# Early idle products, key transposes, a split load of v and reordered ScalarE copies in a fused sketch-attention and GELU kernel

## Chip, cores and metric

The kernel runs on one core of one Trainium2 chip. The metric is the device time of one execution in microseconds (us). A core has TensorE (PE: matrix products and transposes, into PSUM), VectorE (DVE), ScalarE (ACT), GpSimd (POOL) and SyncE (SP, whose queue issues nearly all transfers here). Each engine works through its own instructions in order.

## What is computed

Polynomial-sketch attention on 4 batches x 4 heads x 1088 tokens x 32 features, followed by a two-layer block with exact GELU:

```python
def phi(x):
    a = np.einsum('rd,bhsd->bhsr', S1, x)
    b = np.einsum('rd,bhsd->bhsr', S2, x)
    return np.einsum('bhsi,bhsj->bhsij', a, b).reshape(*x.shape[:-1], r * r)
q_p, k_p = (phi(q), phi(k))                       # r = 8
kv = np.einsum('bhsf,bhsd->bhfd', k_p, v)
z = np.sum(k_p, axis=2)
num = np.einsum('bhsf,bhfd->bhsd', q_p, kv)
den = np.einsum('bhsf,bhf->bhs', q_p, z)[..., None] + 1e-06
x = (num / den)   # heads side by side: 4352 tokens x 128
h = x @ w_in      # 128 x 2048
g = 0.5 * h * (1.0 + erf(h * inv_sqrt2))
out = g @ w_out   # 2048 x 128
```

S1, S2, w_in and w_out arrive as 64-bit floats; the kernel makes 32-bit floats of them itself.

## The kernel before

**Tiling.** Each batch has 1024 main tokens, in two chunks of 512, and 64 remaining tokens. So there are 8 main chunks (n = 0 to 7, batch n // 2) and a ninth chunk of 256 with the remaining tokens of all batches. The hidden width is cut into 16 blocks of 128 (fi). w_in and w_out are held in five pieces of 256, 256, 512, 512 and 512 columns or rows, each with its own transfer and its own rounding.

**Order.** The last lines of the kernel tie every instruction to the one before it on the same engine, so each engine runs in the order of the text. An instruction that waits holds up all that stands behind it on its engine.

**Loads.** SP issues, in order: k of batch 0 in two halves (heads 0 and 2, then 1 and 3), q of chunk 0, v of batch 0 in one load of 512 KB, the remaining tokens' k for batches 0 and 2, the first piece of w_in, the remaining v of batch 0, q of chunk 1, the second piece of w_in, two pieces of w_out. `load_rest` issues all the rest later; its first load of w_in is held back by a one-element memset on POOL (L128).

**Prologue (L511 to L574).** All of batch 0's attention up to the first products is written out by hand:

- `keep_busy(n, ps)` multiplies a tile of zeros (`idle`) into part of a PSUM bank that nobody reads, n times, 256 columns each. These are the idle products. A float32 product shows as two MATMULs in the trace (x2), a transpose as one.
- `Rounding` turns a 64-bit tile into 32 bits: `low_words` (ACT, L209), `fields` (DVE, L213 bits_e and L215 bits_a), `exponents` (ACT, L221), `mantissas` (DVE L229, or with `by_pool` ACT L226 and POOL L227), `signs` (DVE, L234), `product` (L239, on DVE or POOL).
- `key_turn` transposes half of the keys with four PE transposes (L265) and copies them to SBUF (kT, L267, here by ACT). `sketches` transposes the rounded sketch matrices SR (L253) and makes S12, sT (DVE) and Srep (POOL).
- `key_features` multiplies kT by the sketches (L303), copies one factor with ACT (a_t, L316 or L313) and forms the outer products k_p (DVE L317; for one half POOL L314).
- `widen_v(b, r)` copies half of v's heads, those of r, into v_aug (POOL, L278). `kv_sum` accumulates k_p times v_aug (L336), `kv_sum_rem` does so for the remaining tokens (L343), `take_kv` and `turn_kv` give kz (L349, L352, L353).
- `query_turn(n)` makes qT (for chunk 0 with DVE, L367; for chunk 1 with four PE transposes and an ACT copy). `expand_products(n)` is four products of 512 columns (L376) into two pairs of banks; `expand_copy(n, g)`, g = 0 to 3, copies one factor with ACT (A_sb, L383); `expand_multiply(n, i)`, i = 0 or 1, takes copies 2i and 2i+1 and makes half of q_pT with two DVE multiplies (L397).
- `attend_by_token(n, banks)` is 32 small products (L442) of q_pT with kz, the second half of which reads what `expand_multiply(n, 1)` made; then DVE adds (L446), takes reciprocals (L447) and divides (L449) into x_tok. `turn_x` transposes x_tok on PE and copies it to xT.

**Main loop (L641).** A step t belongs to a pair (n, fi). `hidden` multiplies xT by a block of w_in into one of two banks h_ps (L466) and lets ACT take the gelu (g, L468). Two steps later `project` accumulates g times w_out into o_ps (L481). Steps 0 to 3 are fi = 0 to 3 of chunk 0, steps 4 to 7 the same of chunk 1, and so on in turn up to step 31; later chunks run through all 16 blocks each. In between, `slots[t]` holds other work, put there with `at(t, ...)` and run after `hidden` and ahead of `project` of that step. Chunk 1's remaining preparation lies in slots 0 to 3, its `turn_x` ahead of step 4.

Of the kernel before, what the change touches and what calls it, by code (L numbers as in the profile page):

```python
# [16 lines left out]
def kernel(  # L17
# [18 lines left out]
    pe, dve, act, pool, sp = nc.tensor, nc.vector, nc.scalar, nc.gpsimd, nc.sync  # L36
    B, H, S, D = q.shape
# [10 lines left out]
    CW = JC * 128  # L48
# [15 lines left out]
    def work_banks():  # L64

        return wps.tile([128, 2, CW], FP, name="w_ps")

    def work_bank():
        return work_banks()[:, 0]
# [4 lines left out]
    def hidden_bank():  # L74
        return hps.tile([128, CW], FP, name="h_ps")

    def out_bank():
        return ops.tile([128, CW], FP, name="o_ps")


    by_act, by_dve, by_pool = act.copy, dve.tensor_copy, pool.tensor_copy
# [12 lines left out]
    def load_main(eng, n, b, heads=slice(0, H)):  # L94
        eng.dma_start(out=main[n, b][:, heads],  # L95
                      in_=src_of[n][b, heads, 0:MAIN, :].rearrange("h (p j) d -> p h j d", j=J))
# [46 lines left out]
    for r in range(2):  # L143
        load_main(sp, "k", 0, slice(r, H, 2))
    load_q(0)
    load_main(sp, "v", 0)
    load_rem("k", 0)
    load_rem("k", 2)
    load_w_in(0)
# [42 lines left out]
    idle = big.tile([128, 256], FP, name="idle")  # L192
# [58 lines left out]
    def sketches():  # L251
        ps = work_bank()
        pe.transpose(ps[:, :2 * R], in_=SR, identity=ident[:2 * R, :2 * R])  # L253
        dve.tensor_mul(out=S12, in0=ps[:, None, :2 * R].broadcast_to([128, H, 2 * R]),
                       in1=mask4[:, :, None].broadcast_to([128, H, 2 * R]))
        dve.tensor_copy(out=sT, in_=ps[:, :2 * R])
        for i in range(2):
            src = sT[:, 0:R, None] if i == 0 else sT[:, None, R:2 * R]
            pool.tensor_copy(out=Srep[:, i], in_=src.broadcast_to([128, R, R]))
# [10 lines left out]
    def four_tokens(n, b, h, c):  # L270
        return main[n, b][:, h, c * JC:(c + 1) * JC, :].rearrange("p j d -> p (j d)")
# [4 lines left out]
    def widen_v(b, r):  # L276
        to = v_aug.rearrange("p (c r) j (s d) -> p c r j s d", r=2, s=2)[:, :, r, :, r, :]
        pool.tensor_copy(out=to, in_=main["v", b][:, r::2])  # L278
# [9 lines left out]
    def key_turn(b, r, ps, copy):  # L288
        kT[r] = transposed(ps, "kT", [four_tokens("k", b, h, c) for h in (r, r + 2) for c in range(NCH)], copy)
# [7 lines left out]
    def key_features(b, r, banks, by_pool=()):  # L297

        for i in range(2 * NCH):
            for c in range(2):  # L300
                for t in range(2):
                    at = i * 128 + c * 64
                    pe.matmul(banks[t][c * 64:(c + 1) * 64, i * 32:(i + 1) * 32],  # L303
                              lhsT=kT[r][t * 64:(t + 1) * 64, at:at + 64],
                              rhs=S12[t * 64:(t + 1) * 64, 2 * t:2 * t + 2].rearrange("p h r -> p (h r)"),
                              start=True, stop=True)

        k_p[b, r] = att.tile([128, 2, J, R, R], FP, name="k_p")
        a = att.tile([128, 2, J, 2 * R], FP, name="a_t")
        for t in (1, 0):  # L310
            ab = banks[t][:, :128].rearrange("p (n r) -> p n r", r=2 * R)
            if t in by_pool:
                act.copy(out=a[:, t], in_=ab)  # L313
                pool.tensor_mul(**spread(k_p[b, r][:, t], a[:, t, :, 0:R], a[:, t, :, R:2 * R]))  # L314
            else:
                act.copy(out=a[:, t, :, 0:R], in_=ab[:, :, 0:R])  # L316
                dve.tensor_mul(**spread(k_p[b, r][:, t], a[:, t, :, 0:R], ab[:, :, R:2 * R]))  # L317
# [13 lines left out]
    def kv_sum(b, ps, r):  # L331

        for i in range(J):
            ch, t, one = i // 4, i // 2 % 2, i % 2
            for c in range(NP):
                pe.matmul(ps[c * 64:(c + 1) * 64, r * F:(r + 1) * F], lhsT=v_aug[:, 2 * c + r, i, :],  # L336
                          rhs=k_p[b, r][:, t, c * 4 + ch * 2 + one].rearrange("p i j -> p (i j)"),
                          start=(r == 0 and i == 0), stop=False, skip_group_check=True)

    def kv_sum_rem(b, ps):  # L340
        for r in range(2):
            for c in range(NP):
                pe.matmul(ps[c * 64:(c + 1) * 64, r * F:(r + 1) * F], lhsT=v_rem_aug[b][:, 2 * c + r, :],  # L343
                          rhs=k_p_rem[b % 2][:, 2 * c + r].rearrange("p i j -> p (i j)"),
                          start=False, stop=True, skip_group_check=True)
# [13 lines left out]
    def query_turn(n, copy=by_act):  # L359


        if n == 1:
            turned = transposed(out_bank(), "qT", [q_sb[1][:, h].rearrange("p j d -> p (j d)") for h in range(H)], copy)
            qT[n] = turned.rearrange("p (h j t) -> p h j t", h=H, j=JC)
            return
        qT[n] = att.tile([128, H, width[n] // 128, D], FP, name="qT" if n < NMAIN else "qT_rem")
        dve.transpose(out=qT[n], in_=q_sb[n] if n < NMAIN else rem["q"].rearrange("p i h d -> p h i d"))  # L367
# [12 lines left out]
    def expand_copy(n, g):  # L380
        if g % 2 == 0:
            A[g // 2] = att.tile([128, 2, CW], FP, name="A_sb", bufs=2)
        act.copy(out=A[g // 2][F:, g % 2, :width[n]], in_=B_of[n][g // 2][:F, g % 2, :width[n]])  # L383
# [48 lines left out]
    def attend_by_token(n, banks):  # L432

        x_tok[n] = att.tile([128, JC, H, D], FP, name="x_tok", bufs=1)
        to = x_tok[n].rearrange("p j (c r) d -> p (j c) r d", r=2)
        den = att.tile([128, 2, JC * NP], FP, name="den_tok")
        for i in range(JC):
            for c in range(NP):
                for half in range(2):
                    for r in range(2):  # L440
                        rows, at, tok = slice(r * F, (r + 1) * F), (i * NP + c) * C, i * 128 + half * 64
                        pe.matmul(banks[r][half * 64:(half + 1) * 64, at:at + C], lhsT=qp[n][rows, c, tok:tok + 64],  # L442
                                  rhs=kz[n // NCH][rows, c, (0, D - 1)[r]:(C, 2 * D)[r]], start=True, stop=True)
        nd = [banks[r][:, :JC * NP * C].rearrange("p (g c) -> p g c", c=C) for r in range(2)]
        for r in range(2):
            dve.tensor_scalar(out=den[:, r], in0=nd[r][:, :, (D, 0)[r]], scalar1=1e-6, scalar2=None, op0=AX.add)  # L446
        dve.reciprocal(out=den, in_=den)  # L447
        for r in range(2):
            dve.tensor_mul(out=to[:, :, r], in0=nd[r][:, :, r:r + D],  # L449
                           in1=den[:, r, :, None].broadcast_to([128, JC * NP, D]))  # L450

    def turn_x(n, ps, copy):
        xT[n] = transposed(ps, "xT", [x_tok[n][:, j].rearrange("p h d -> p (h d)") for j in range(JC)], copy)
# [50 lines left out]
                         in_=oT[c * 32:(c + 1) * 32].rearrange("p n (m d) -> p (n m) d", d=32))  # L504


    def keep_busy(n, ps):
        for i in range(n):
            pe.matmul(ps[:, 256:512], lhsT=idle[:, 0:128], rhs=idle, start=True, stop=True)

    keep_busy(3, work_bank())  # L511
    r = Rounding(SR)
    r.low_words()
    r.fields()
    r.exponents()
    r.finish()
    key_turn(0, 0, hidden_bank(), by_act)
    sketches()
    query_turn(0)
    key_turn(0, 1, hidden_bank(), by_act)  # L520
    widen_v(0, 0)
    banks = [out_bank(), out_bank()]
    key_features(0, 0, banks)
    key_features(0, 1, [hidden_bank(), hidden_bank()], by_pool=(1,))
    widen_v(0, 1)
    widen_v_rem(0)
    expand_products(0)
# [10 lines left out]
    expand_copy(0, 3)  # L538
    expand_multiply(0, 1)
    kv_sum(0, kv_bank, 1)  # L540
    kv_sum_rem(0, kv_bank)
    w_in[0].exponents()
    take_kv(0, kv_bank, by_act)
# [9 lines left out]
    w_in[0].product(pool)  # L553
    w_in[1].low_words()
    w_in[1].exponents()
    keep_busy(1, hidden_bank())
    attend_by_token(0, [hidden_bank(), hidden_bank()])
    expand_products(1)
    keep_busy(1, out_bank())
    w_out = [Rounding(w) for w in w_out_sb[:2]]  # L560
    w_out[0].low_words()
    for g in range(2):
# [3 lines left out]
    w_in[1].product(pool)  # L566
    w_out[0].fields()
    turn_x(0, hidden_bank(), by_act)
    w_out[0].exponents()
    expand_multiply(1, 0)  # L570
    w_out[0].mantissas()
    w_out[0].signs()
    w_out[0].product(pool)
    w_out[1].fields()  # L574


    steps = [(n, fi) for f in range(0, NF, 4) for n in range(2) for fi in range(f, f + 4)]
# [3 lines left out]
    def at(t, f, *a):  # L581
        slots[t].append(lambda: f(*a))
# [25 lines left out]
        at(t, lambda: (r.append(Rounding(w)), r[0].low_words(), r[0].fields()))  # L608
        at(t + 1, lambda: (r[0].exponents(), r[0].finish()))

    at(0, lambda: (w_out[1].low_words(), w_out[1].exponents()))
    for g in range(2, 4):
        at(1, expand_copy, 1, g)
    at(1, expand_multiply, 1, 1)
    at(1, lambda: (w_out[1].mantissas(), w_out[1].signs(), w_out[1].product(pool)))
    at(3, lambda: attend_by_token(1, halves(work_banks())))
    for i, (t0, t1) in enumerate(((4, 6), (8, 10), (12, 20))):
        round_at(t0, w_in_sb[i + 2])
# [76 lines left out]
```

## Time and profile before

| | |
|---|---|
| runs | 294.57, 294.48, 296.11, 293.99 us; median 294.53 |
| profiled execution | 294.38 us |
| its span | 292.1 us |
| busy in the span | PE 282.5 us (97%), ACT 135.0 (46%), DVE 120.6 (41%), POOL 15.0 (5%) |
| granted PE clock | 0.998 of full speed on average |

The span is the time from the first to the last recorded instruction. PE is nearly always busy, so where it was idle matters. In stretches of the span (us), from the view that gives each engine's busy time by window:

| stretch | PE busy | DVE busy | ACT busy | POOL busy | transfer share |
|---|---|---|---|---|---|
| 0 to 3 | 1.80 | 1.75 | 1.27 | 1.78 | 0.34 |
| 3 to 6 | 2.48 | 1.78 | 1.31 | 0.04 | 0.86 |
| 6 to 9 | 2.67 | 2.28 | 1.55 | 1.04 | 0.98 |
| 9 to 12 | 2.70 | 2.93 | 2.88 | 2.00 | 0.82 |
| 12 to 15 | 2.24 | 2.80 | 1.37 | 0.00 | 0.00 |
| 15 to 18 | 2.66 | 2.36 | 2.84 | 1.83 | 0.23 |
| 18 to 21 | 2.55 | 2.92 | 1.64 | 0.55 | 0.96 |
| 21 to 24 | 2.83 | 1.52 | 2.92 | 0.54 | 0.99 |
| 24 to 27 | 2.15 | 2.87 | 0.22 | 0.72 | 1.06 |
| 27 to 30 | 2.33 | 0.36 | 1.28 | 0.00 | 1.10 |
| 30 to 33 | 3.00 | 1.37 | 1.92 | 1.54 | 0.79 |

The transfer share is the mean busy share of the 16 transfer engines (overlapping packets can put it over 1). TensorE's waits, summed by who ended them, are all in the first 29 us:

```text
PE w_ps L509 <- DVE idle L193: 1.2, 1, 1.2
PE o_ps L343 <- DVE k_p_rem L329: 1.0, 1, 1.0
PE h_ps L466 <- POOL w_in L239: 0.8, 1, 0.8
PE h_ps L466 <- ACT xT L267: 0.7, 1, 0.7
PE w_ps L253 <- DVE SR L239: 0.5, 1, 0.5
PE w_ps L265 <- DVE x_tok L449: 0.5, 1, 0.5
PE w_ps L442 <- DVE q_pT L397: 0.3, 1, 0.3
```

Each line names the instruction that waited, the one it waited for, and then the total, the number and the longest of these waits in us. A line such as `16.53 0.70 PE L509 MATMUL ... x2` in a timeline gives start, duration, engine, line, operation, what it writes and reads, and how many instructions are merged in it; square brackets name the idle time before it and its cause.

### The profile page before, as it was taken

How to read it: one execution, taken by the hardware profiler on the slowest of the kernel's cores; microseconds unless marked ns; L12 is line 12 of the kernel's file. 1: busy time of each engine (PE TensorE's matmuls, PEld its weight loads, DVE VectorE, ACT ScalarE, POOL GpSimd, SP SyncE). 2: the span in 40 equal slices, each digit the busy share in tenths (PEclk: the TensorE clock that was granted, in tenths of full speed). 3: DMA queues.
4: the chain of work that ended last, by engine and by line, in shares of the span. 5: the costliest groups of instructions: out<-in, count | busy, mean ns of one | idle time of the engine just before them, and what ended most of it. 6: DMA issues, size and time to landing. Idle time of an engine off the chain costs nothing.

```text
span 292.1 us, 3792 instructions
## 1 busy us (share of the span) xinstructions
PE 282.5 (97%) x1497; PEld 137.2 (47%) x1497; DVE 120.6 (41%) x186; ACT 135.0 (46%) x259; POOL 15.0 (5%) x45
## 2 busy tenths in 40 slices
PE   7887999999999999999999999999999999999994
PEld 5543445543443345533443345533443344444694
DVE  5985586344813284251713085242513161222000
ACT  4673674265435443256335543256336533443341
POOL 2340200110000000200000000000000000000000
PEclk9999999999999999999999999999999999999999
DMA  6569678100012000200002000200001000200010
GB/s 196 181 180 375 125 202 225 20 0 0 2 27 34 12 0 2 36 2 0 0 0 37 0 2 0 39 0 0 0 9 29 0 0 0 36 2 0 9 29 18
DMA packets 32561, 13.37 MB, mean 46 GB/s; under 512 B 21408, under 2 KB 31904, under 8 KB 32544
## 3 DMA queue, kind: packets, MB, share of 16 engines
q1 hardware_dynamic: 32304, 13.05, 17.3%
q8 instruction: 12, 0.20, 0.3%
q10 hardware_dynamic: 240, 0.08, 0.1%
q14 instruction: 5, 0.04, 0.0%
HBM read 10.90 MB, written 2.23 MB: 45 GB/s over the span
## 4 chain that ended last, share of the span: by engine, by line
PE 90%; DVE 4%; DMA 2%; SPq 1%; issue 1%; ACT 1%; ACTq 0%
PE h_ps L466 39%; PE o_ps L481 38%; PE o_ps L478 2%; PE w_ps L376 2%; PE w_ps L417 2%; PE w_ps L336 2%; DMA raw_w_in<-in_moe_w_in_dram 2%; DVE q_pT L397 1%; PE w_ps L265 1%; PE w_ps L303 1%; DVE bits_a L215 0%; SPq L95 0%; SPq L108 0%; PE h_ps L442 0%; DVE bits_e L234 0%
## 5 line engine op out<-in xcount | busy, mean ns | idle before, releaser
L468 ACT ACTIVATE g<-h_ps 128x512 f32<-128x512 f32 (+1 forms) x144 | 82.4, 573 | 130.3 <-PE h_ps L466 130.0
L466 PE MATMUL h_ps<-xT,w_in 128*128 128x512 f32 (+1 forms) x288 | 140.3, 569 | 1.5 <-POOL w_in L239 0.8
L481 PE MATMUL o_ps<-g,w_out 128*128 128x512 f32 x256 | 133.1, 601 | 0.2 <-POOL w_out L239 0.2
L466 PEld LDWEIGHTS h_ps<-xT,w_in 128*128 128x128 f32 x288 | 53.5, 190 | 63.9 <-issue 60.3
L481 PEld LDWEIGHTS o_ps<-g,w_out 128*128 128x128 f32 x256 | 46.2, 190 | 58.1 <-issue 56.5
L424 DVE RECIPROCAL den<-den 128x512 f32<-128x512 f32 (+1 forms) x7 | 21.9, 3124 | 44.0 <-ACT den L423 44.0
L397 DVE TENSOR_TENSOR q_pT<-A_sb,w_ps 64x512 f32<-64x512 f32 x32 | 22.1, 691 | 25.4 <-ACT A_sb L383 24.8
L491 DVE STREAM_TRANSPOSE oT<-o_ps 128x512 f32<-128x512 f32 x8 | 5.7, 717 | 43.9 <-PE o_ps L481 43.9
L383 ACT COPY A_sb<-w_ps 64x512 f32<-64x512 f32 (+1 forms) x36 | 17.7, 557 | 3.4 <-PE w_ps L376 3.2
L428 DVE TENSOR_TENSOR xT<-w_ps,den 32x512 f32<-32x512 f32 (+1 forms) x28 | 18.2, 649 | 1.0
L423 ACT ACTIVATE den<-w_ps 32x512 f32<-32x512 f32 (+1 forms) x28 | 15.6, 557 | 3.0 <-PE w_ps L417 2.7
L317 DVE TENSOR_TENSOR k_p<-a_t,w_ps 128x512 f32<-128x512 f32 x12 | 8.0, 686 | 6.5 <-ACT a_t L316 6.5
L478 PEld LDWEIGHTS o_ps<-w_out,g 128*128 128x128 f32 x64 | 9.3, 191 | 0.7
L278 POOL COPY v_aug<-v 128x512 f32<-128x512 f32 x8 | 4.9, 618 | 91.0 <-issue 62.0
L478 PE MATMUL o_ps<-w_out,g 128*128 128x128 f32 x64 | 9.4, 274 | 0.0
L376 PE MATMUL w_ps<-qT,Srep 32*128 32x512 f32 x64 | 9.1, 639 | 0.2 <-DVE qT L367 0.2
L229 DVE SCALAR_TENSOR_TENSOR bits_m<-bits_a,bits_low 128x512 f32<-128x512 uint32 (+2 forms) x10 | 5.7, 572 | 3.7 <-ACT bits_low L209 3.1
L417 PE MATMUL w_ps<-q_pT,kz 64*64 64x512 f32 (+1 forms) x80 | 7.2, 458 | 0.0
L221 ACT ACTIVATE bits_r<-bits_e,below 128x512 uint32<-128x512 uint32 (+2 forms) x11 | 6.7, 609 | 0.6 <-DVE bits_e L213 0.5
L336 PEld LDWEIGHTS w_ps<-k_p,v_aug 128*64 128x64 f32 x192 | 5.8, 138 | 2.3 <-issue 2.3
L336 PE MATMUL w_ps<-k_p,v_aug 128*64 128x64 f32 x192 | 6.3, 224 | 0.0
L267 DVE COPY kT<-w_ps 128x512 f32<-128x512 f32 x6 | 3.9, 685 | 4.5 <-PE w_ps L265 4.5
(119 smaller groups left out, 113.2 us busy)
## 6 DMA issues: line engine op xcount, KB each, us to landing
v<-in_v_dram SPq DMA_DIRECT2D x4, 512.0 KB, 6.8
raw_w_in<-in_moe_w_in_dram SPq DMA_DIRECT2D x3, 512.0 KB, 4.5
raw_w_out<-in_moe_w_out_dram SPq DMA_DIRECT2D x3, 512.0 KB, 7.5
k<-in_k_dram SPq DMA_DIRECT2D x3, 512.0 KB, 6.0
q<-in_q_dram SPq DMA_DIRECT2D x24, 64.0 KB, 4.7
out_dram<-oT SPq DMA_DIRECT2D x24, 64.0 KB, 2.2
k<-in_k_dram SPq DMA_DIRECT2D x2, 256.0 KB, 3.1
q<-in_q_dram SPq DMA_DIRECT2D x2, 256.0 KB, 4.9
```

The costliest lines, as they stand in the source:

```text
L336: pe.matmul(ps[c * 64:(c + 1) * 64, r * F:(r + 1) * F], lhsT=v_aug[:, 2 * c + r, i, :], rhs=k_p[b, r][:, t, c * 4 + ch * 2 + one].rearrang ...
L376: pe.matmul(B_of[n][g // 2][:, g % 2, :W], lhsT=Srep[rows].rearrange("p a i j -> p (a i j)"), rhs=qT[n][rows].rearrange("p h j t -> p (h j ...
L383: act.copy(out=A[g // 2][F:, g % 2, :width[n]], in_=B_of[n][g // 2][:F, g % 2, :width[n]])
L397: dve.tensor_mul(out=cols[r * F:(r + 1) * F], in0=a[:, :, r::2], in1=b[:, :, r::2])
L417: pe.matmul(banks[r][c * F:(c + 1) * F, c0:c1], lhsT=kz[b][r * F:(r + 1) * F, c, :], rhs=qp[n][r * F:(r + 1) * F, c, c0:c1], start=True, s ...
L423: act.activation(out=den[h * D:(h + 1) * D, :W], in_=banks[r][at:at + D, :W], func=ACT.Copy, bias=1e-6)
L424: dve.reciprocal(out=den[:, :W], in_=den[:, :W])
L428: dve.tensor_mul(out=xT[n][rows, :W], in0=banks[h % 2][rows, :W], in1=den[rows, :W])
L466: pe.matmul(ps[:, :W], lhsT=w_tile(w_in_sb, fi), rhs=xT[n][:, :W], start=True, stop=True)
L468: act.activation(out=g_of[n, fi][:, :W], in_=ps[:, :W], func=ACT.Gelu)
L478: pe.matmul(o_of[n][:, i * 128:(i + 1) * 128], lhsT=g[:, i * 128:(i + 1) * 128], rhs=w_tile(w_out_sb, fi), start=(first and i == 0), stop= ...
L481: pe.matmul(o_of[n], lhsT=w_tile(w_out_sb, fi), rhs=g, start=first, stop=final)
```

## The change

Five things are changed; the function bodies not shown stay as they are.

1. v of batch 0 is loaded in two transfers, heads 0 and 2 first, so that each is what one `widen_v` reads.
2. `key_turn(0, 1)` moves from behind `query_turn(0)` to ahead of `sketches()`.
3. `keep_busy` can take fewer columns. Three idle products of 128 columns come in around `key_features`, one of 256 ahead of `kv_sum_rem`; the one ahead of chunk 0's attention shrinks to 128, the one behind `expand_products(1)` becomes two, and one more follows the transposes of `turn_x(0)`.
4. ACT's copies g = 2 and 3 for chunk 1 move from step 1, behind two gelus: copy 2 into the prologue, copy 3 into step 0, behind the first gelu. The multiply that takes both moves to step 0.
5. The first piece of w_out takes its last product on DVE instead of POOL, directly behind its mantissas and signs. The second piece's low words move into the prologue, its fields and exponents to step 1, its mantissas, signs and product (POOL) to step 2.

```diff
     load_q(0)
-    load_main(sp, "v", 0)
+    for r in range(2):
+        load_main(sp, "v", 0, slice(r, H, 2))
     load_rem("k", 0)
...
-    def keep_busy(n, ps):
+    def keep_busy(n, ps, cols=256):
         for i in range(n):
-            pe.matmul(ps[:, 256:512], lhsT=idle[:, 0:128], rhs=idle, start=True, stop=True)
-
-    keep_busy(3, work_bank())
+            pe.matmul(ps[:, CW - cols:], lhsT=idle[:, 0:128], rhs=idle[:, :cols], start=True, stop=True)
+
+    bank = work_bank()
+    keep_busy(3, bank)
...
     key_turn(0, 0, hidden_bank(), by_act)
+    key_turn(0, 1, hidden_bank(), by_act)
     sketches()
+    keep_busy(1, bank, 128)
     query_turn(0)
-    key_turn(0, 1, hidden_bank(), by_act)
     widen_v(0, 0)
     banks = [out_bank(), out_bank()]
     key_features(0, 0, banks)
+    keep_busy(1, bank, 128)
     key_features(0, 1, [hidden_bank(), hidden_bank()], by_pool=(1,))
+    keep_busy(1, bank, 128)
     widen_v(0, 1)
...
     kv_sum(0, kv_bank, 1)
+    keep_busy(1, hidden_bank())
     kv_sum_rem(0, kv_bank)
...
-    keep_busy(1, hidden_bank())
-    attend_by_token(0, [hidden_bank(), hidden_bank()])
+    banks = [hidden_bank(), hidden_bank()]
+    keep_busy(1, banks[0], 128)
+    attend_by_token(0, banks)
     expand_products(1)
-    keep_busy(1, out_bank())
+    bank = out_bank()
+    keep_busy(2, bank)
...
     turn_x(0, hidden_bank(), by_act)
+    keep_busy(1, bank)
     w_out[0].exponents()
+    expand_copy(1, 2)
     expand_multiply(1, 0)
-    w_out[0].mantissas()
-    w_out[0].signs()
-    w_out[0].product(pool)
-    w_out[1].fields()
+    w_out[0].finish()
+    w_out[1].low_words()
...
-    at(0, lambda: (w_out[1].low_words(), w_out[1].exponents()))
-    for g in range(2, 4):
-        at(1, expand_copy, 1, g)
-    at(1, expand_multiply, 1, 1)
-    at(1, lambda: (w_out[1].mantissas(), w_out[1].signs(), w_out[1].product(pool)))
+    at(0, expand_copy, 1, 3)
+    at(0, expand_multiply, 1, 1)
+    at(1, lambda: (w_out[1].fields(), w_out[1].exponents()))
+    at(2, lambda: (w_out[1].mantissas(), w_out[1].signs(), w_out[1].product(pool)))
```

## The prediction

> **What bounds the kernel now.** I read the page's chain of waits by engine first, then the same chain cut to the first 31 us, then the timelines of the engines there.
>
> ```profile
> PE 90%; DVE 4%; DMA 2%; SPq 1%; issue 1%; ACT 1%; ACTq 0%
> ```
>
> TensorE (PE) sets the end for 90% of the span. The other 10% lie ahead of 28.15 us: from there PE goes from product to product with no idle time, so whatever brings that moment forward brings the end forward by as much. This is the chain before it:
>
> ```profile
> 4.34 4.87 DMA raw_w_in<-in_moe_w_in_dram
> ...
> 10.04 0.69 DVE bits_a L215
> 10.73 0.03 issue
> 10.76 0.69 DVE q_pT L397
> ...
> 13.90 0.43 PE h_ps L509 x2
> 14.34 1.25 PE h_ps L442 x64
> ...
> 21.04 0.51 ACT bits_r L221
> 21.55 0.48 ACT g L468
> 22.05 1.07 ACT A_sb L383 x2
> 23.12 0.02 issue
> 23.14 0.69 DVE q_pT L397
> ...
> 28.15 1.12 PE h_ps L466 x2
> ```
>
> Columns are start, duration and what ran. Up to 18.5 us VectorE (DVE) decides, with TensorE and ScalarE (ACT) in between. At 21 to 23 us chunk 1's last two copies (A_sb, L383) stand on ACT behind a rounding step (L221), which itself waited for DVE, and behind a gelu (L468). The multiply of chunk 1 (L397) waits for them, attention (L442) for that, then x_tok, its transposes, xT and the product at 28.15.
>
> The POOL and DVE timelines show the second thing:
>
> ```profile
> 8.32 0.61 POOL L278 COPY v_aug<-v 128x512 f32<-128x512 f32 x1 [1.96 <-DMA v<-in_v_dram]
> 8.90 1.07 POOL L314 TENSOR_TENSOR k_p<-a_t 128x512 f32<-128x512 f32 x1
> 9.91 0.67 POOL L278 COPY v_aug<-v 128x512 f32<-128x512 f32 x1
> ```
> ```profile
> 9.22 0.89 DVE L213 TENSOR_SCALAR bits_e<-raw_w_in 128x256 uint32<-128x256 uint32 x1
> ...
> 14.43 0.29 DVE L213 TENSOR_SCALAR bits_e<-raw_w_in 128x256 uint32<-128x256 uint32 x1
> ```
>
> The same field operation takes 0.89 us while POOL works and 0.29 us at 14.43 while POOL rests. It ends at 10.11, 0.14 after POOL's k_p ends (9.97); bits_a (0.69) ends at 10.73, 0.15 after the v_aug copy. So POOL's late start, which waited 1.96 us for v, costs DVE about 0.9 us.
>
> **1. v in two loads, and the early part.** v is issued at 2.33 and lands 5.9 us later, 8.23; q lands at 6.65. The transfer engines are 98% busy from 6 to 9 us. The first half of v should land midway between, near 7.4. POOL then copies until 8.05, starts k_p there instead of at 8.90 (its input a_t from ScalarE is there at 7.77) and ends it at 9.1; the second v copy runs to 9.75. The field operations still cannot start before 9.22 (DVE is busy until 9.21, and w_in's first piece lands then): bits_e ends 0.14 after POOL's copy, 9.89, and bits_a, partly beside two short copies, near 10.3. The next multiply also needs the second A_sb copy, 9.64 to 10.2, some 0.1 later because an idle product of 128 columns (half of the 0.43 in the chain: 0.21) stands before expand_products. It starts at 10.35 instead of 10.76: **-0.41**.
>
> The price is one more issue on SP's queue. v's took 0.51 and the gap 0.04, so k_rem, w_in, v_rem, q of chunk 1 and all behind them are issued 0.55 later. With the transfer engines full the same bytes land at the same time (cost 0); at worst w_in lands 0.55 later, at 9.76, and DVE idles. Nearest row: 98% busy, so I take 0. The worst end, w_in late and both field operations still blocked (1.5 us), puts the multiply at 11.27, **+0.5**; the best is -0.46, when DVE waits for ScalarE alone. What follows (k_p_rem, L343, kv, attention of chunk 0, x_tok) moves by the same amount, since each waits for that DVE chain.
>
> The Trainium skill, "SBUF — State Buffer", "Who interferes with whom", has VectorE's two-port tensor_scalar and GpSimd exclude each other for a whole instruction, whoever issues first. Rows and rule agree on the 0.6 us; by the rule, losing the race to the second v copy would again cost all of it, and the early gain would be about nothing.
>
> **2. Key transposes first.** k's second half, issued at 1.25, lands 3.4 us later, 4.65. Four transposes (0.66 with the drain) fit ahead of the sketches' transpose, which waits for SR until 5.25. ScalarE's second kT copy then ends near 6.0 instead of 6.68, which removes 0.07 of idle time on PE; the idle product there takes it back. DVE starts k_p at 7.36 because of qT anyway: **0**. Bounds: -0.1 and, should k be late, the rival below.
>
> **3. Idle products.** Those after the sketches (0.21 in 0.5 of waiting), ahead of kv_sum_rem (0.43 in 0.97) and after turn_x (0.43 in 0.78) fill waits that stay: 0. The one ahead of chunk 0's attention shrinks from 0.43 to 0.21, but that attention waits for kz (14.21): 0. One doesn't fit:
>
> ```profile
> 16.53 0.70 PE L509 MATMUL o_ps<-idle 128*128 128x256 f32 x2
> 17.06 0.60 PE L265 MATMUL h_ps<-ident,x_tok 128*128 128x128 f32 x4
> 18.45 2.97 PE L466 MATMUL h_ps<-xT,w_in 128*128 128x512 f32 x6 [0.78 <-POOL w_in L239]
> 21.60 1.12 PE L481 MATMUL o_ps<-g,w_out 128*128 128x512 f32 x2 [0.17 <-POOL w_out L239]
> ```
>
> Here there are now two. x_tok is ready at 16.89 and the transposes begin at 17.06; two products from 16.53 end at 16.53 + 0.86 = 17.39. Transposes, xT and the first product come **+0.33** later (bounds 0 and 0.43). Nothing hides it: xT ends at 18.31, and PE starts at 18.45.
>
> As to their use: the first three products took 2.93 us, 0.98 each, against 0.43 for one at 13.90, so the array starts slow; but from 5.3 us on equal shapes keep equal speed, and the longest wait later is 0.97. The Trainium skill, "TensorE: Matmul & The Clock Gate", "Why this matters for your kernels", asks for no idle gap over about 3 us. By that rule the new products protect nothing and only the 0.33 is left of them; no row here shows a drop that they could prevent.
>
> **4. Chunk 1's copies among the first gelus.** Let t0 be the first product (18.45 before). ScalarE: xT ends at t0 - 0.14; then exponents, A_sb copy 2, low words (0.51, 0.53, 0.43, less overlaps) to t0 + 1.2; the first gelu (0.60) to t0 + 1.8; copy 3 to t0 + 2.33; the second gelu to t0 + 2.9. PE: the third product needs the first gelu's bank, t0 + 1.85 (before: 20.29, t0 + 1.84), no change. The first projection waited until 21.60 = t0 + 3.15 for POOL's product; DVE now does it itself right after mantissas and signs. DVE starts the multiply near t0 - 0.23 and needs 1.41 + 0.43 + 0.34 + 0.42 (a 128x512 product there took 0.69, half is 0.35; the 128x256 row of L229 0.43): t0 + 2.4. PE itself is free at t0 + 2.71: 0.44 won. Then the fourth product to t0 + 4.43. The second multiply runs from t0 + 2.4 to t0 + 3.83, so chunk 1's attention no longer waits: 1.26 us, done at t0 + 5.69. Before:
>
> ```profile
> 24.61 0.66 PE L442 MATMUL w_ps<-kz,q_pT 64*64 64x33 f32 x30 [0.34 <-DVE q_pT L397]
> ```
>
> that is 25.27 = t0 + 6.82: **-1.13**. Behind the multiply DVE still has w_out's second piece (0.22 + 0.36 + 0.42 + 0.34), done at t0 + 5.2, ahead of den_tok; ScalarE's exponents wait for its fields (t0 + 4.1), with the third and fourth gelu queued behind, done at t0 + 5.9. Who needs those is chunk 1's first product at t0 + 8.57 and later. From attention's end to that product it stays 28.15 - 25.27 = 2.88 us. Bounds: -0.6 if DVE's field operations are stretched to 0.83 each as at 17.69 and den_tok waits for them; -1.4 if the wait for the first gelu vanishes too.
>
> After that the loop is unchanged. Its nearest due time is w_in's third piece, made by 33.83 and used near 35.1; its steps follow the loop's slots and shift along.
>
> **Sum.** -0.41 + 0.33 - 1.13 = -1.21. The profiled execution took 294.38 us (span 292.1 plus 2.3 around it), 0.15 under the median of 294.53: 294.38 - 1.21 = **293.2**. Its own range, from the bounds without their worst coincidence: 292.6 to 293.9.
>
> **Rivals.** (a) More is won: the unprofiled runs spread from 293.99 to 296.11 with nothing in this trace to explain it. If it is the slow start of the array lasting longer in some, the added products cut it, and the 0.54 between median and lowest run comes on top: 294.53 - 1.21 - 0.54 = 292.8. For it: the half speed until about 4 us. Against: one trace can't show it.
> (b) The extra issue undoes the early part: w_in or k_rem land 0.55 later and POOL still blocks DVE: +0.5 in place of -0.41, 294.1. For it: k_rem lands at 8.68 and PE wants it at 8.80; w_in lands just as DVE comes free. Against: full transfer engines.
> (c) Slower: PE, in order, is stuck at the second key transposes. The sketches, both features and DVE's chain stand behind them, and lateness counts one for one. It begins to cost when k's half lands after 4.8, reaches the path 0.27 later (a_t ready 7.09, k_p 7.36), and eats the gain beyond 6.3; landing as late as q's 6.65 gives 294.38 + 0.37 = 294.7, and 1.5 slower needs 7.8. Against: 4.65 in this trace.
>
> **How the numbers follow.** Forecast 0.60, (a) 0.18, (b) 0.15, (c) 0.07. What a measurement here can tell from no change is about 0.5%, 1.47 us, so faster means below 293.06. That takes (a) and 0.22 of the forecast: 0.40. Slower, above 296.0, is most of (c): 0.06. The rest, 0.54, is the same. The range reaches from under (a) to past (b): 292.3 to 294.5.
>
> **What would show it.** In the changed kernel: k_p on POOL starts near 8.05; the first L397 near 10.35; two idle products in a row ahead of x_tok's transposes with these 0.3 late; the fourth A_sb copy between the first two gelus; no wait of L442 on q_pT; chunk 1's first product near 26.9 instead of 28.15. I am wrong if that product doesn't come earlier by about as much as the end does, if w_in's landing moves the field operations past 9.6, or if the loop shows idle time on PE after it.

## The result, and the profile after

The changed kernel takes 293.75 us (median of 54 executions, 293.08 to 297.11), the kernel before 294.18 (78 executions, 293.60 to 297.65). The ratio is 0.9972, 95% interval 0.996 to 0.9983: 0.28% faster. The interval lies clear of 1, but the gain is less than the half per cent from which the prediction counted a change, and its 0.43 us are about a third of the 1.21 us that the prediction worked out.

The medians hide half of it. Both kernels have late executions, 1.5 us or more above their fastest: 19 of 78 before, 2 of 54 after. So the mean falls by 0.83 us (294.61 to 293.78) where the median falls by 0.43.

The profiled execution of the changed kernel is one of its two late ones (297.06 us, span 295.0). Its early PE timeline, columns as before:

```profile
6.70 1.08 PE L304 MATMUL o_ps<-S,kT 64*64 64x32 f32 x32
7.71 0.79 PE L510 MATMUL w_ps<-idle 128*128 128x128 f32 x2
8.44 1.08 PE L304 MATMUL h_ps<-S,kT 64*64 64x32 f32 x32
9.45 0.79 PE L510 MATMUL w_ps<-idle 128*128 128x128 f32 x2
10.17 2.21 PE L377 MATMUL w_ps<-qT,Srep 32*128 32x512 f32 x8
...
12.71 1.78 PE L337 MATMUL o_ps<-k_p,v_aug 128*64 128x64 f32 x32
...
```

The same kernel profiled again, in a usual execution (293.66 us, span 291.5):

```profile
6.39 0.67 PE L304 MATMUL o_ps<-S,kT 64*64 64x32 f32 x32
6.99 0.49 PE L510 MATMUL w_ps<-idle 128*128 128x128 f32 x2
7.41 0.67 PE L304 MATMUL h_ps<-S,kT 64*64 64x32 f32 x32
8.01 0.49 PE L510 MATMUL w_ps<-idle 128*128 128x128 f32 x2
8.42 1.25 PE L377 MATMUL w_ps<-qT,Srep 32*128 32x512 f32 x8
...
9.87 1.15 PE L337 MATMUL o_ps<-k_p,v_aug 128*64 128x64 f32 x32
```

Equal work at little more than half the pace: 2.21 against 1.25 us for L377, 1.78 against 1.15 for L337, during which the pace changes. In the late execution the half pace, with which every profiled execution starts, lasts until about 14.4 us; in the usual one until about 5.7. The clock column of the window view doesn't show it; for 9 to 12 us of the late execution it says 1.00 (window, its length, then the busy time of PE, weight loads, DVE, ACT and POOL with their instructions, the clock, the transfer share, GB/s):

```profile
9.00:12.00 3.00, 3.00 (x30) 1.51 (x26) 2.15 (x4) 0.38 (x2) 2.04 (x4) 1.00 0.71 242
```

So the usual execution is what can be compared with the profile before. Its chain of waits (start, duration, what ran) up to chunk 1's first product:

```profile
5.78 0.59 ACT kT L268
6.38 0.01 issue
6.39 0.67 PE o_ps L304 x32
7.06 0.42 PE w_ps L510 x2
7.48 0.60 PE h_ps L304 x32
8.07 0.42 PE w_ps L510 x2
8.49 1.19 PE w_ps L377 x8
...
14.60 1.14 PE h_ps L443 x64
15.73 1.07 PE w_ps L377 x8
16.80 1.06 PE o_ps L510 x4
17.86 0.45 PE h_ps L266 x4
...
19.07 1.95 PE h_ps L467 x4
...
23.84 1.11 PE w_ps L443 x64
...
27.67 1.12 PE h_ps L467 x2
```

Before, the early part of this chain was a load and DVE's operations. Now it is PE, with the idle products (L510) themselves on it. At the marks that the prediction used:

| mark | before | after (usual) | moved in this stretch | predicted |
|---|---|---|---|---|
| first q_pT multiply on DVE (L397, now L398) | 10.76 | 11.10 | +0.34 | -0.41 |
| chunk 0's first product (L466, now L467) | 18.45 | 19.07 | +0.28 | +0.33 |
| chunk 1's first product | 28.15 | 27.67 | -1.10 | -1.13 |
| sum | | | -0.48 | -1.21 |

From there to the end nothing changed: about 263.9 us before, 263.8 after. Two of three stretches came as predicted; the first went the other way.

The table sets one execution of each kernel against one of the other. For the last two stretches that is enough. In the profiles of the experiments below, chunk 0's first product to chunk 1's takes 8.60 to 8.64 us wherever the copies have moved (9.70 before). First multiply to chunk 0's first product takes 7.67 to 7.69 with one idle product ahead of x_tok's transposes and 7.96 or 7.97 with two, but for two executions with two (8.64 in experiment 3, 8.68 in the late one). The first mark is not so firm: with the early part of the kernel before, unchanged, it lay at 10.76 here and at 9.94 in experiment 8; with that of the changed kernel at 11.10 here and at 10.68 in experiment 4. So the +0.34 can't be read as the price of the change in this stretch; the experiments have to give that.

### The profile page after: what moved, and what is told of

It is laid out like the page before. It is cut to its first block, busy times and chain, and to the rows that moved or that the text cites. A ratio compares the mean times of both kernels' runs of the same rounds, so it can differ in the third digit from the quotient of the medians.

```text
span 295.0 us, 3815 instructions
## 1 busy us (share of the span) xinstructions
PE 288.3 (98%) x1509; PEld 141.7 (48%) x1509; DVE 121.0 (41%) x187; ACT 135.1 (46%) x259; POOL 15.2 (5%) x44
## 4 chain that ended last, share of the span: by engine, by line
PE 97%; DVE 1%; ACT 1%; issue 0%
PE h_ps L467 40%; PE o_ps L482 38%; PE w_ps L377 3%; PE o_ps L479 2%; PE w_ps L418 2%; PE w_ps L337 2%; PE w_ps L510 2%; PE w_ps L266 1%; PE w_ps L304 1%; PE o_ps L337 1%; PE h_ps L266 1%; ACT xT L268 0%; PE h_ps L443 0%; PE w_ps L443 0%; PE o_ps L510 0%; PE h_ps L304 0%
## 5 line engine op out<-in xcount | busy, mean ns | idle before, releaser
L467 PE MATMUL h_ps<-xT,w_in 128*128 128x512 f32 (+1 forms) x288 | 140.4, 569 | 1.0 <-ACT xT L268 1.0
L467 PEld LDWEIGHTS h_ps<-xT,w_in 128*128 128x128 f32 x288 | 53.5, 190 | 63.6 <-issue 60.4
L398 DVE TENSOR_TENSOR q_pT<-A_sb,w_ps 64x512 f32<-64x512 f32 x32 | 22.1, 691 | 26.0 <-ACT A_sb L384 25.3
L377 PE MATMUL w_ps<-qT,Srep 32*128 32x512 f32 x64 | 10.2, 702 | 0.0
L337 PEld LDWEIGHTS w_ps<-k_p,v_aug 128*64 128x64 f32 x192 | 5.8, 138 | 2.3 <-issue 2.3
L510 PE MATMUL w_ps<-idle 128*128 128x256 f32 (+1 forms) x12 | 5.3, 581 | 1.2 <-DVE idle L194 1.2
L337 PE MATMUL w_ps<-k_p,v_aug 128*64 128x64 f32 x192 | 6.3, 224 | 0.0
```

What stands on the lines that cost most here:

```text
L377: pe.matmul(B_of[n][g // 2][:, g % 2, :W], lhsT=Srep[rows].rearrange("p a i j -> p (a i j)"), rhs=qT[n][rows].rearrange("p h j t -> p (h j ...
L398: dve.tensor_mul(out=cols[r * F:(r + 1) * F], in0=a[:, :, r::2], in1=b[:, :, r::2])
L467: pe.matmul(ps[:, :W], lhsT=w_tile(w_in_sb, fi), rhs=xT[n][:, :W], start=True, stop=True)
```

## Experiments

Edits are against the changed kernel unless said otherwise. "Low" is the median of the executions that are not late. The kernel before, run beside them in three batches, had 294.01, 293.90 and 294.12 by that measure, and 27 late of 104.

**1. The changed kernel again.**

> The changed kernel once more, for a profile of one of its usual executions: the one shown took 297.06 us, 3.3 above its own median of 293.75, and in it every early product ran at half pace until 14.4 us. Theory A (clock start): this half pace is no part of the change; a usual execution shows the fast pace (one 128x256 product 0.43 us, four transposes 0.66) from some point before 6 us, and a span near 291.6. Theory B (the change moved the early part back for good): the usual execution also has half pace to about 14 us and the gain comes later. By my sum chunk 1's first product starts near 26.9 in a usual execution; if the early part did not gain, near 27.4 to 27.7.

Measured: 293.70 us, none late of 12, ratio 0.9981 (0.9964 to 0.9998). Chunk 1's first product at 27.67. The long half pace is no fixed part of the change (theory A), but the early part did not gain. DVE, POOL and ACT of this execution show why not:

```profile
9.19 0.55 DVE L214 TENSOR_SCALAR bits_e<-raw_w_in 128x256 uint32<-128x256 uint32 x1
9.66 0.69 DVE L216 TENSOR_SCALAR bits_a<-raw_w_in 128x256 uint32<-128x256 uint32 x1
11.10 1.40 DVE L398 TENSOR_TENSOR q_pT<-A_sb,w_ps 64x512 f32<-64x512 f32 x2 [0.75 <-ACT A_sb L384]
```
```profile
8.52 1.07 POOL L315 TENSOR_TENSOR k_p<-a_t 128x512 f32<-128x512 f32 x1 [0.72 <-ACT a_t L314]
9.53 0.67 POOL L279 COPY v_aug<-v 128x512 f32<-128x512 f32 x1
```
```profile
9.60 0.58 ACT L384 COPY A_sb<-w_ps 64x512 f32<-64x512 f32 x1 [1.05 <-PE w_ps L377]
```

DVE ends its field operations at 10.35, 0.38 earlier than before (10.73). The split load should give that, but this pair doesn't show it: with one load they ended at 9.90 in experiment 8. Then DVE idles 0.75 us for a copy of ScalarE's, which waited 1.05 us for PE. The first wait removed was followed by another, made by PE.

**2. The idle products of before.**

```diff
     sketches()
-    keep_busy(1, bank, 128)
...
     key_features(0, 0, banks)
-    keep_busy(1, bank, 128)
     key_features(0, 1, [hidden_bank(), hidden_bank()], by_pool=(1,))
-    keep_busy(1, bank, 128)
...
-    keep_busy(1, hidden_bank())
     kv_sum_rem(0, kv_bank)
...
-    banks = [hidden_bank(), hidden_bank()]
-    keep_busy(1, banks[0], 128)
-    attend_by_token(0, banks)
+    keep_busy(1, hidden_bank())
+    attend_by_token(0, [hidden_bank(), hidden_bank()])
...
-    keep_busy(2, bank)
+    keep_busy(1, bank)
...
     turn_x(0, hidden_bank(), by_act)
-    keep_busy(1, bank)
```

> The changed kernel with the idle products of before (three at the start, one of 256 ahead of chunk 0's attention, one behind the second expand_products; none of the added ones). Theory A (the added idle products keep the slow pace from lasting): executions 1.5 us or more above the lowest come back, about 1 in 4 as in the kernel before (19 of 78), against 2 of 54 with the change; the usual execution is about 0.3 to 0.4 us faster than the changed kernel's, since the second product ahead of x_tok's transposes is gone: main cluster near 293.3. Theory B (the added products do nothing but cost time): as few late executions as the changed kernel, and 0.3 to 0.4 faster.

Measured: median 292.50, low 292.13, 5 late of 12 (294.2 to 294.8). Repeated, as a control for the ninth experiment:

> The kernel with the idle products of before once more, beside the fitted one on the same chip: lower cluster 292.0 to 292.6 and 3 to 6 late of 12 if the 5 of 12 were typical. If the fitted products shorten the half pace, the fitted version has fewer late executions than this one; if they do nothing, as many.

Measured: median 293.81, low 292.53, 6 late of 12. The usual execution is 1.2 to 1.6 us faster than the changed kernel's, far more than the 0.3 to 0.4 expected, and 11 of 24 are late. So the added idle products do both: they cost a good us in the usual execution and, with the keys first, make late ones rare (with the keys back 4 of 12 are late: experiment 6).

**3. Without the three early products only.**

```diff
     sketches()
-    keep_busy(1, bank, 128)
...
     key_features(0, 0, banks)
-    keep_busy(1, bank, 128)
     key_features(0, 1, [hidden_bank(), hidden_bank()], by_pool=(1,))
-    keep_busy(1, bank, 128)
```

> The changed kernel without the three idle products around key_features; the other added ones stay. Theory A (weight loads): each of these products takes TensorE 0.42 us and not 0.21, two of them stand on the path sketches - features - expand_products - A_sb copies - first multiply of DVE, so the usual execution gains 0.6 to 0.85 us: main cluster 292.6 to 293.0; and the executions of 1.5 us or more above the lowest return (about 1 in 3). Theory B (they fill waits, prediction's step 3): no change of the main cluster, 293.1 to 294.1.

Measured: low 292.59 against 293.70, 3 late of 12. Theory A holds in direction and place; the gain, 1.1 us, is above its 0.6 to 0.85. The PE timeline of this kernel and its first multiply on DVE:

```profile
5.27 0.23 PE L254 MATMUL w_ps<-ident,SR 16*128 16x16 f32 x1
5.97 0.67 PE L304 MATMUL o_ps<-S,kT 64*64 64x32 f32 x32 [0.48 <-DVE sT L257]
6.43 0.68 PE L304 MATMUL h_ps<-S,kT 64*64 64x32 f32 x32
7.04 1.14 PE L377 MATMUL w_ps<-qT,Srep 32*128 32x512 f32 x8
...
14.59 0.44 PE L443 MATMUL h_ps<-kz,q_pT 64*64 64x33 f32 x16 [0.48 <-issue]
```
```profile
9.72 1.40 DVE L398 TENSOR_TENSOR q_pT<-A_sb,w_ps 64x512 f32<-64x512 f32 x2 [0.16 <-ACT A_sb L384]
```

and that of the kernel of the next experiment, which has the three products and whose sketches were transposed at the same moment:

```profile
5.26 0.23 PE L254 MATMUL w_ps<-ident,SR 16*128 16x16 f32 x1
5.42 0.49 PE L510 MATMUL w_ps<-idle 128*128 128x128 f32 x2
5.97 0.67 PE L304 MATMUL o_ps<-S,kT 64*64 64x32 f32 x32
6.57 0.49 PE L510 MATMUL w_ps<-idle 128*128 128x128 f32 x2
6.99 0.67 PE L304 MATMUL h_ps<-S,kT 64*64 64x32 f32 x32
7.58 0.49 PE L510 MATMUL w_ps<-idle 128*128 128x128 f32 x2
8.00 1.26 PE L377 MATMUL w_ps<-qT,Srep 32*128 32x512 f32 x8
```
```profile
10.68 1.40 DVE L398 TENSOR_TENSOR q_pT<-A_sb,w_ps 64x512 f32<-64x512 f32 x2 [0.75 <-ACT A_sb L384]
```

The first product is free: the features start at 5.97 with or without it, after the 0.48 wait for the sketches. The other two put expand_products off from 7.04 to 8.00, and DVE's first multiply from 9.72 to 10.68, both by 0.96.

Between these two executions the 0.96 doesn't reach the end; both took 293.07 us. The one without the products idles 0.48 us inside chunk 0's attention (at 14.59 above, for a reason that the trace doesn't show), and the other has one product less later on. The first lies 0.48 above its kernel's low, the second 0.65 below its own. So the traces give the place and the 0.96, and the lows give the 1.1.

**4. One product ahead of x_tok's transposes.**

```diff
-    keep_busy(2, bank)
+    keep_busy(1, bank)
```

> The changed kernel with one idle product instead of two ahead of x_tok's transposes. Prediction's step 3: 0.33 us faster, main cluster 292.8 to 293.8. Rival: the transposes wait for x_tok anyway and nothing changes.

Measured: low 293.72, 1 late of 12, ratio to before 0.9982 (0.9953 to 1.0011): by the times no difference can be seen. By the traces, from the start of chunk 0's attention to chunk 0's first product it takes 14.18 to 18.35, 4.17 us, against 14.60 to 19.07, 4.47, with two products. The 0.30 of the prediction is there in that stretch, but in the times it is not shown.

**5. The early products twice as wide.**

```diff
     sketches()
-    keep_busy(1, bank, 128)
+    keep_busy(1, bank)
...
     key_features(0, 0, banks)
-    keep_busy(1, bank, 128)
+    keep_busy(1, bank)
     key_features(0, 1, [hidden_bank(), hidden_bank()], by_pool=(1,))
-    keep_busy(1, bank, 128)
+    keep_busy(1, bank)
```

> The changed kernel with the three idle products around key_features widened from 128 to 256 columns. Theory A (loading the weights sets the time of a narrow product): a product of twice the columns takes TensorE little longer, 0.43 to 0.55 us against 0.42, and the usual execution moves by 0 to 0.25 us. Theory B (the columns set the time, and something else made the 0.42): each takes 0.2 us more, two of them on the path: +0.4 to +0.6 us.

Measured: low 294.18, 0.48 above the changed kernel, none late of 10. PE timeline:

```profile
7.54 0.70 PE L510 MATMUL w_ps<-idle 128*128 128x256 f32 x2
8.17 0.67 PE L304 MATMUL h_ps<-S,kT 64*64 64x32 f32 x32
8.77 0.70 PE L510 MATMUL w_ps<-idle 128*128 128x256 f32 x2
9.39 0.70 PE L377 MATMUL w_ps<-qT,Srep 32*128 32x512 f32 x2
...
```

From an idle product's start to the next real one it is 0.63 and 0.62 us here, 0.42 and 0.41 at half the width. Theory A falls: columns do count, 0.21 us for 128 more, and the 0.48 lies in theory B's range. But on top of the columns comes a fixed 0.21 us. That is close to the 0.19 us that one weight load of these products takes in the trace, which suggests the weight loads as its cause and doesn't show it. Placed between small products of other weights, a product of 128 columns costs 0.42, not half of a 256-column product's 0.43.

**6. The second key transposes back in their place.**

```diff
-    key_turn(0, 1, hidden_bank(), by_act)
     sketches()
...
     query_turn(0)
+    key_turn(0, 1, hidden_bank(), by_act)
```

> The changed kernel with the second key transposes back behind the sketches and the first query turn. Prediction's step 2: no difference (within 0.1 us). Rival: in the changed kernel four more transposes stand ahead of the sketches' transpose while the array still runs at half pace, so the sketches come 0.3 to 0.5 us late and all of DVE's chain with them; then this kernel is 0.2 to 0.5 us faster, and its sketch transpose starts near 5.2 instead of later.

Measured: low 293.64 against 293.70, 4 late of 12 (297.1 to 298.2). The transposes move the usual execution by nothing: the sketches do come earlier (5.33 against 5.67), but PE then does the transposes itself before the features, which start at 6.35 against 6.39. (The 5.67 isn't fixed either: with the keys first, experiments 3 and 4 have the sketches at 5.27 and 5.26, as the half pace ended sooner there.) With the idle products of before it is the same:

> The kernel with the idle products of before and the split load, and the second key transposes back behind the sketches. Prediction's step 2 (order of the keys is worth nothing): lower cluster as with the keys first, 292.0 to 292.5. Rival (keys first delays the sketches while the array is at half pace): lower cluster 0.2 to 0.4 lower. Rival (keys first closes the wait for SR and so ends the half pace sooner): more late executions here than the 5 of 12 there.

(This kernel is the second experiment's with the same edit.) Measured: low 292.57 against 292.13 and 292.53, 4 late of 12. What the order may change is the share of late executions: with the keys back 4 of 12 against 2 of 66 for the changed kernel (54 and 12 executions), with the added products in both. With the old products, 4 of 12 against 11 of 24, no such effect shows.

**7. v in one load again** (on the kernel of the second experiment).

```diff
-    for r in range(2):
-        load_main(sp, "v", 0, slice(r, H, 2))
+    load_main(sp, "v", 0)
```

> The kernel with the idle products of before (its lower cluster 292.03 to 292.54), and also v in one load again. Prediction's step 1: the split is worth 0.4 us where DVE sets the pace, so the lower cluster moves to 292.4 to 292.9. Rival (the split is worth nothing): the lower cluster stays at 292.0 to 292.5, and the key order or chance made the difference to the kernel with the copies alone (292.3 to 292.9).

Measured: low 292.84 against 292.13 and 292.53, so the split is worth 0.3 to 0.7 us where PE doesn't hold DVE up. With the keys in their old place two kernels differ in the load alone too, that of experiment 8 (one load, low 292.68) and the second one of experiment 6 (two loads, 292.57): 0.1. One late of 12, against 11 of 24 with two loads; whether the load has to do with that is not settled.

**8. ScalarE's copies and w_out's order alone** (the kernel before with parts 4 and 5 of the change).

```diff
+    expand_copy(1, 2)
     expand_multiply(1, 0)
...
+    at(0, expand_copy, 1, 3)
+    at(0, expand_multiply, 1, 1)
...
```

> The kernel before with the reordered ScalarE copies and the first two w_out pieces' new order alone (no new idle products, one load of v, keys in the old place). Prediction's step 4: -1.13 us against before, main cluster near 293.0, with the late executions as frequent as before. Rival (the wait goes elsewhere): less than half of that, as x_tok's division or w_out's second piece becomes the next wait.

Measured: low 292.68, 2 late of 12, ratio 0.9956 (0.9937 to 0.9975); the kernel before had low 294.01 beside it. That is -1.33 us. This part alone does more than the whole change. Its chain:

```profile
9.94 0.69 DVE q_pT L397
...
17.62 1.96 PE h_ps L466 x4
...
26.25 1.12 PE h_ps L466 x2
```

From chunk 0's first product to chunk 1's it is 8.63 against 9.70 us, so -1.07 of the -1.33 is in the stretch where the edit is. The first multiply comes 0.82 earlier than in the profile before, with no edit ahead of it. Why the medians differ by 0.26 more than the stretch is open.

**9. A version with the idle products that fit.**

```diff
     key_features(0, 0, banks)
-    keep_busy(1, bank, 128)
     key_features(0, 1, [hidden_bank(), hidden_bank()], by_pool=(1,))
-    keep_busy(1, bank, 128)
...
-    keep_busy(2, bank)
+    keep_busy(1, bank)
```

> A version made to beat both: the changed kernel with only the idle products that fit a wait: after the sketches, ahead of kv_sum_rem, ahead of chunk 0's attention, one instead of two ahead of x_tok's transposes, one behind them. Theory A: lower cluster as with the idle products of before, 292.0 to 292.6, with late executions less frequent than there (5 of 12). Theory B (only the unbroken row of products up to 8.4 us keeps the half pace short): as many late executions as there.

Measured: median 292.58, low 292.38, 2 late of 11. Repeated:

> The fitted version once more, for the share of late executions and a firmer interval: lower cluster 292.0 to 293.0 and 1 to 4 late of 12, if the first measurement (2 of 11 late) was typical; 0.994 of the time before.

Measured: median 292.72, none late of 12, ratio to before 0.9932 (0.9907 to 0.9956). Over both, 23 executions have a median of 292.69, 1.06 below the changed kernel's 293.75, and 2 are late, against 11 of 24 with the idle products of before. This version beats both kernels.

## Why the prediction held, and where it missed

293.75 lies in the range of 292.3 to 294.5, 0.55 above the 293.2, and "the same", at 0.54 the likeliest, came. In part that is luck. The gain was 0.43 instead of 1.21 us in the median, and 0.48 instead of 1.21 between the marks of the two profiles. The range is 2.2 us wide, and the execution that the sum started from (294.38) lay 0.20 above the median of 78, so 0.78 of missing gain shows as a miss of less than 0.6.

**Copies among the gelus (step 4): right.** -1.10 in the stretch against -1.13 predicted, -1.06 to -1.10 in all profiles with the copies moved, and -1.33 in the times of the kernel that has this part alone. L443 waited for nothing in the usual execution, and attention ended 5.84 us after chunk 0's first product (predicted 5.69).

**v in two loads (step 1): the waits were read rightly, the size is not settled.** In the usual execution POOL's k_p starts at 8.52 instead of 8.90 and DVE's fields end 0.38 earlier; w_in's later issue (4.84 instead of 4.34) delays nothing, so rival (b) did not come. But with one load k_p started at 8.07 in experiment 8, so these 0.38 may be chance. In the times the split alone is worth 0.1 to 0.7, which has the predicted 0.41 in it. In the changed kernel DVE waits for ScalarE instead. The prediction named that wait as the next one, but put the multiply at 10.35, not 11.10.

The Trainium skill's "SBUF — State Buffer", "Who interferes with whom", still fits: bits_e now ends at 9.74, 0.15 after POOL's k_p (8.52 + 1.07), and bits_a at 10.35, 0.15 after the second v copy (9.53 + 0.67). bits_a lost that race in full, 0.69 as before; bits_e took 0.55 instead of 0.89. So losing to the second v copy cost bits_a's part of the gain, and not all of it as the prediction had it.

**Key transposes first (step 2): right.** 0 predicted; putting them back gave -0.06 us with the added products, +0.04 and +0.44 against two measurements of the kernel without them. In the profiled usual execution the sketches' transpose did come at 5.67 instead of 5.25: SR was ready at 5.11, and eight transposes at half pace (1.83 us) stood ahead of it. k's second half kept nobody waiting, so rival (c), which needed that, did not come.

**Idle products (step 3): this is the step that failed.** "Those after the sketches ... fill waits that stay: 0" costed one of the three. The second was set against a wait of 0.07 us (step 2), and the third put at some 0.1 us on a copy of ScalarE's that was not to set the pace (step 1). The price of one was also mis-sized, 0.21 taken as half of the 0.43 that the chain before shows for a product of 256 columns, where 0.42 was measured. The two put the first multiply off by 0.96 between executions whose sketches were transposed at the same moment, and cost 1.1 in the times. Without the three the kernel's low is 292.59 against 293.90 for the kernel before beside it: a gain of 1.31, close to the predicted 1.21. The pair ahead of x_tok's transposes was right: +0.28 against +0.33.

**Their use was wrong too.** "No row here shows a drop that they could prevent" was true of the one trace, but 46 of 182 executions of the kernel before are late and 2 of 66 of the changed one. All four late executions that were profiled (one of the changed kernel, two in experiment 2, one in 7; none of the kernel before) show the array at half pace, until 14.4 us in the first and 10.4 to 10.8 in the others; in the ten usual ones it was over by 7.4. Rival (a) had this mechanism, at 0.18, and put it on the median, where it isn't; it lies in the mean. The Trainium skill's "TensorE: Matmul & The Clock Gate", "What's actually happening", says that the array starts at half rate and is let go after sustained activity. The two paces agree with that. The section's table puts the activity needed at about 3.4 us; the late trace of the changed kernel doesn't fit that, as PE was busy for all of the 12.00 us from 3 to 15 and at half pace until 14.4. Why the half pace ends so late in some executions was not settled. Nor is it shown which of the added products makes late executions rarer, or whether they do so without the keys first.

## What to carry to other kernels

An idle product is free only inside a wait that is longer than its full price (here 0.42 us, not 0.21); measure that price between the very instructions it goes between, not in a stream of its own kind. Look at the spread of many executions before judging filler work from one trace: what it buys can be rarer late executions, and what it costs falls on all of them. When several edits go in together, run each alone: here one edit was worth three times the whole. Before two profiles are subtracted, look how far a mark moves between executions of the same code: here by 0.4 to 0.8 us, as much as the effect sought.

## What the runs showed of the hardware

- The array can run at half pace until 13 us after its first product, with PE busy all the time from 3 us on, while the profile's granted clock says 1.00. Here only the durations of equal instructions gave it away (L377: 2.21 against 1.25 us).
- How long this lasts differs between executions of one kernel: until 14.4 us in one that took 297.06 us and until 5.7 in one of 293.66. The times of the kernel before fall into separate clusters too, 293.5 to 294.8 and 295.3 upward, but none of its late executions was profiled.
- A lone idle product between small ones cost 0.42 us at 128 columns and 0.63 at 256. The second of two in a row of 256 columns added 0.43 (start to next start 16.73 to 17.70 in experiment 1 with two, 16.31 to 16.85 in experiment 4 with one).
